# A planned attention and channel-mix kernel: longer warm-up of TensorE, two small loads requested elsewhere, a finer last piece, and a new order

## The chip, the core and the metric

The kernel runs on one core of one Trainium2 chip. The metric is the device time of one execution in microseconds (us). Three executions of the kernel before took 245.69, 247.63 and 247.31 us; their median is 247.31 us. A further execution was taken with the profiler; it took 246.16 us, of which the profile's span covers 244.4 us.

A core has five engines that run side by side, each through its own queue in order: PE (TensorE, the matmuls; its weight loads are listed as PEld), DVE (VectorE), ACT (ScalarE), POOL (GpSimd) and SP (SyncE, which here only requests transfers). They wait for each other through semaphores. Transfers run on 16 DMA engines of their own. PSUM, where matmuls write, has eight banks of 512 fp32 columns.

## The reference

Two layers, for 4 batches of 768 rows.

1. **Hashed attention**, 8 heads of 64 columns. `proj` (64 x 6) gives each row of q and k six sign bits, `bits = (q @ proj > 0)`. A row of q sees only rows of k whose six bits are the same: `scores = where(same, q @ k.T / 8, -1e9)`, `attn = softmax(scores)`, `x = attn @ v`. The heads side by side make 512 columns.
2. **Channel mix.** `xk = mu_k * x + (1 - mu_k) * x_prev`, `xr` likewise with `mu_r`, where `x_prev` is x one row earlier. `out = sigmoid(xr @ w_r) * (relu(xk @ w_k)^2 @ w_v)`, with w_k 512 x 1024, w_v 1024 x 512, w_r 512 x 512. The output is 4 x 768 x 512 in fp32.

## The kernel before, in words

**Units of work.** Two heads of one batch make a pair, so there are 16 pairs, `n` = 0 to 15, four to a batch. For a pair, q and k are loaded, scaled and split into a high and a low fp16 half (`hi`, `lo` on DVE: L456 and L461 for pairs 0 and 1, L393 and L396 for the others), and transposed. Pairs 0 and 1 are transposed by PE against the identity `idh` (`t...`, L474) and copied out of PSUM (`evt...`, L479 on DVE, L481 on ACT); the others are transposed by a DMA (L400, requested by SP).

**Hash bits.** `proj` is loaded into `pj` (L260). POOL makes `npj = -pj` (L261), the fp16 high part `p1` (two copies, L264) and the low part `p2` (two subtractions, L267). PE multiplies the transposed rows with `p1` and `p2`: in two halves for the first head of pair 0 (`b0...`, L494), else a pair at a time (`bits...`, L420). The signs become six extra rows of the transposed q and k: `beb...` for the first head of pair 0 (L500 on ACT for k, L502 on DVE for q), else `bx` on DVE (L423) and then a copy by POOL (`row...`, L440). With them the score matmul itself tells equal from unequal bits.

**Scores and values.** `sc{n}_{s}` (L533) is one of nine steps of 1024 score columns of a pair; ACT takes its exponential (`exp{n}_{s}`, L537, 144 in all). `oo{n}_{j}` (L560, with L555 for pairs 0 to 3) multiplies by v; DVE divides (`rc`, `ob`, L571 to L578). The result is transposed into `xt` and mixed on DVE (`df`, `xka`, `xk`, `xra`, `xr`, L598 to L633). The sums over v are POOL's (`vsum`, L351 to L357), and so are the casts of v for pairs 0 to 3 (`va`, L345) and of the weights to bf16 (`wc`, L303).

**Channel mix of a batch**, after its four pairs: `kp` (L648) with a relu on ACT (L652) and a square on DVE (L655); `r` (L668) with a tanh on ACT (L671); then, for each of six chunks of 128 rows, `v` (L681), the product on DVE (`os`, L688), and the store, requested by SP (`st`, L691). The last chunk of the last batch is done in two pieces of 256 columns, each with its own matmuls, product and store.

**Order.** Every step is recorded by `add(engine, duration, function, ...)` and numbered in the order of the calls. The list `ORDER` holds these numbers in the order in which the steps are issued; an engine runs its own steps in that order. `BANKS` gives the PSUM bank of each step that takes one. Both lists are written out in the file. The durations and due times (`dur`, `at`, `svc`) in the `add` calls are not used when the program is built from these lists.

In the numbering of the kernel before, 0 is the zeroing of `wz`, 2 to 8 are seven warm-up matmuls of 512 columns (L246), 10 and 11 make the identities `idh` and `idb` (two POOL instructions each), 12 to 24 are POOL's memsets, 25 requests `pj` on ACT's queue, and 26 to 30 are the five POOL steps that make `npj`, `p1` and `p2`. POOL's steps start in the order 18, 13, 20, 12, 14, 11, 19, 10, 1, 15, 26, 27, 28, 29, 30; then comes `va0`.

Of the kernel before, what the change touches and what calls it, by code (L numbers as in the profile page):

```python
# [13 lines left out]
ALU = mybir.AluOpType  # L14
# [113 lines left out]
def kernel(  # L128
# [19 lines left out]
    P = 128  # L148
# [6 lines left out]
    NPB = H // 2  # L155
    NPAIRS = B * NPB

    NWARM = 7
    NUC = 4
    FIRST = {(n, side, j): ("DVE", "DVE", None) for n in range(2) for side in "qk" for j in range(2)}  # L160
    FIRST[(0, "q", 0)] = ("DVE", "DVE", "DVE")
# [534 lines left out]
    for n in range(NPAIRS):  # L696
        if n == 0:
            for m in range(2):
                add_load(m)
# [48 lines left out]
```

## Time and profile before

| what | value |
|---|---|
| three executions | 245.69, 247.63, 247.31 us (median 247.31) |
| the profiled execution | 246.16 us; span 244.4 us |
| busy: PE, DVE, ACT, POOL | 233.1, 189.4, 180.7, 103.8 us |
| first exponential on ACT | 14.12 us |
| PE's last matmuls begin | 239.21 us |
| last product on DVE | 241.16 us, 0.42 us long |
| `pj` requested, landed | 1.17 us, 4.0 us later |

The profile lists, for one execution, when each engine ran what. Times are counted from the start of the span. "Idle before" is the time that an engine stood still ahead of an instruction, and the name behind the arrow is what ended it. A line of the timeline stands for several instructions of one form in a row; its second number reaches from the first's start to the last's end. Matmuls overlap, so a line of PE is about 0.17 us longer than the work in it, and lines overlap by as much.

### The profile page before, as it was taken

The page shows a single profiled execution, that of the slowest core. Times are in us where ns is not written, and L with a number is a line of the kernel's source. Part 1 is how long each engine was busy: PE and PEld are TensorE (multiplying, and loading weights), DVE is VectorE, ACT ScalarE, POOL GpSimd, SP SyncE. Part 2 cuts the span into 40 slices and gives each one's busy share as a digit, 9 for nine tenths or more (in the row PEclk, how much of TensorE's full clock was granted, in tenths as well). Part 3 has the DMA queues.
Part 4 walks back from the last instruction along what each step waited for, and adds up shares of the span by engine and source line. Part 5 has one row for each costly group of instructions (what it writes and reads, how often), then busy time and mean ns, then how long its engine had stood idle before and what let it go on. Part 6 is the DMA issues. An engine that isn't in the chain of part 4 may idle for free.

```text
span 244.4 us, 6114 instructions
## 1 busy us (share of the span) xinstructions
PE 233.1 (95%) x2461; PEld 140.5 (57%) x2461; DVE 189.4 (77%) x392; ACT 180.7 (74%) x241; POOL 103.8 (42%) x151
## 2 busy tenths in 40 slices
PE   6899998999999989999999999999999999999994
PEld 3455565675666645555766665565557575455443
DVE  3998779899997999997898989975246837873342
ACT  3469999899999895688887886886979970156320
POOL 3479989599947694116087030770040000000000
PEclk9999999999999999999999999999999999999999
DMA  7999999999999999999999794265102101321033
GB/s 228 343 248 189 242 249 186 343 198 362 291 248 245 265 376 195 178 278 325 187 198 238 203 200 135 60 160 120 32 1 89 32 3 35 129 85 45 3 130 129
DMA packets 72381, 43.99 MB, mean 180 GB/s; under 512 B 54816, under 2 KB 67360, under 8 KB 72352
## 3 DMA queue, kind: packets, MB, share of 16 engines
q1 hardware_dynamic: 72128, 43.40, 72.7%
q8 instruction: 19, 0.31, 0.6%
q10 hardware_dynamic: 224, 0.20, 0.3%
q14 instruction: 10, 0.08, 0.1%
HBM read 24.12 MB, written 6.29 MB: 124 GB/s over the span
## 4 chain that ended last, share of the span: by engine, by line
PE 60%; DVE 1%; issue 0%
PE ps_all L681 16%; PE ps_all L648 13%; PE ps_all L533 13%; PE ps_all L560 8%; PE ps_all L668 8%; PE ps_all L420 2%; DVE tm L630 0%; DVE os L688 0%; DVE ob L578 0%; PE ps_all L369 0%; PE ps_all L588 0%; PE ps_all L370 0%
## 5 line engine op out<-in xcount | busy, mean ns | idle before, releaser
L537 ACT ACTIVATE pt<-ps_all 128x1024 bf16<-128x1024 f32 x144 | 140.6, 1041 | 22.4 <-PE ps_all L533 21.4
L533 PE MATMUL ps_all<-a 128*128 128x256 f16 (+1 forms) x384 | 82.0, 326 | 0.5
L440 POOL COPY a<-bx 6x384 f32<-6x384 f32 x62 | 45.3, 731 | 58.2 <-DVE bx L423 35.1
L648 PE MATMUL ps_all<-xk,wk 128*128 128x384 bf16 x256 | 48.8, 326 | 0.1
L560 PEld LDWEIGHTS <-pt 128*128 128x128 bf16 x1152 | 43.2, 97 | 9.5 <-issue 1.4
L681 PE MATMUL ps_all<-wv,k 128*128 128x512 bf16 (+1 forms) x200 | 46.7, 370 | 0.8 <-DVE ob L578 0.8
L533 PEld LDWEIGHTS <-a 128*128 128x128 f16 x384 | 32.8, 97 | 24.2 <-issue 5.5
L560 PE MATMUL ps_all<-va,pt 128*128 128x65 bf16 x1152 | 45.3, 193 | 0.0
L655 DVE TENSOR_TENSOR k<-kr 128x384 bf16<-128x384 bf16 x64 | 24.8, 404 | 15.5 <-ACT kr L652 13.3
L652 ACT ACTIVATE kr<-ps_all 128x384 bf16<-128x384 f32 x64 | 30.0, 500 | 9.0 <-PE ps_all L648 7.2
L648 PEld LDWEIGHTS <-wk 128*128 128x128 bf16 x256 | 24.6, 98 | 17.2 <-POOL wk L303 0.4
L681 PEld LDWEIGHTS <-k 128*128 128x128 bf16 x200 | 19.0, 98 | 19.3 <-issue 1.1
L671 ACT ACTIVATE rs<-ps_all 128x512 f32<-128x512 f32 x24 | 14.3, 603 | 21.2 <-PE ps_all L668 17.8
L396 DVE SCALAR_TENSOR_TENSOR nh<-nat,nh 128x1536 f16<-128x1536 f32 (+1 forms) x16 | 26.6, 1662 | 0.3
L668 PE MATMUL ps_all<-wr,xr 128*128 128x512 bf16 x96 | 24.5, 379 | 0.2 <-DVE ob L578 0.2
L688 DVE SCALAR_TENSOR_TENSOR os<-rs,ps_all 128x512 f32<-128x512 f32 (+1 forms) x25 | 16.5, 661 | 9.8 <-PE ps_all L681 9.3
L423 DVE TENSOR_SCALAR bx<-ps_all 128x768 uint16<-128x768 uint16 (+1 forms) x16 | 15.2, 952 | 5.2 <-PE ps_all L420 4.3
L351 POOL TENSOR_TENSOR vt<-vn 128x384 f32<-128x384 f32 x12 | 15.0, 1253 | 8.3 <-DMA vn<-in_v_dram 7.7
L578 DVE TENSOR_TENSOR ob<-ps_all,rc 128x384 bf16<-128x384 f32 x32 | 17.3, 548 | 0.4
L393 DVE TENSOR_SCALAR nh<-nat 128x1536 f16<-128x1536 f32 (+1 forms) x16 | 15.3, 959 | 1.4 <-DMA nat<-in_q_dram 1.4
L420 PE MATMUL ps_all<-a,p 128*32 128x512 f16 (+1 forms) x248 | 14.2, 334 | 1.7 <-DMA a<-nh 0.8
L668 PEld LDWEIGHTS <-xr 128*128 128x128 bf16 x96 | 9.2, 98 | 10.4 <-issue 0.8
(72 smaller groups left out, 179.7 us busy)
## 6 DMA issues: line engine op xcount, KB each, us to landing
vn<-in_v_dram SPq DMA_DIRECT2D x16, 384.0 KB, 5.4
out_dram<-os SPq DMA_DIRECT2D x23, 256.0 KB, 2.2
nat<-in_q_dram SPq DMA_DIRECT2D x15, 384.0 KB, 5.3
nat<-in_k_dram SPq DMA_DIRECT2D x15, 384.0 KB, 5.1
wst<-in_moe_w_k_dram SPq DMA_DIRECT2D x2, 512.0 KB, 6.4
wst<-in_moe_w_r_dram SPq DMA_DIRECT2D x2, 512.0 KB, 4.3
wst<-in_moe_w_v_dram SPq DMA_DIRECT2D x2, 512.0 KB, 6.0
k<-in_moe_w_k_dram SPq DMA_DIRECT2D x1, 512.0 KB, 4.8
```

The lines of the kernel that those rows point to most:

```text
L396: nc.vector.scalar_tensor_tensor(out=nh[:, :, D:P], in0=nat.rearrange("p j (c d) -> p (j c) d", d=D), scalar=QS, in1=nh[:, :, 0:D], op0=AL ...
L420: nc.tensor.matmul(ps[32 * i : 32 * i + 32, lo:hi], w_, side_a[side][sa][:, j, lo:hi], start=st, stop=not st)
L440: nc.gpsimd.tensor_copy(side_a[side][sa][D : D + NB, j, :].bitcast(FP32), bx_t[sx][32 * i : 32 * i + NB, :].bitcast(FP32))
L533: nc.tensor.matmul(ps[:, lo - s * STEP : hi - s * STEP], side_a["k"][sa][:, j, jc * P : (jc + 1) * P], side_a["q"][sa][:, j, q0 : q0 + hi ...
L537: nc.scalar.activation(out=pt_t[sp][:, s * STEP : (s + 1) * STEP], in_=ps_t[plan.slot[nm]], func=AF.Exp, bias=EBIAS, scale=ESC)
L560: nc.tensor.matmul(oo[:, ic * 65 : ic * 65 + 65], pt_t[sp][:, o : o + P], va_t[sa][:, j, jc, 0 : D + 1], start=(not uc and ic == 0 and jc ...
L578: nc.vector.tensor_tensor(out=ob_t[so][:, :, j * D : (j + 1) * D], in0=oo[:, :, 0:D], in1=rc_t[sr][:, 1, :].unsqueeze(2).to_broadcast([P, ...
L648: nc.tensor.matmul(ps[:, 0:HALF], wk_sb[:, d, fc * P : (fc + 1) * P], xk_t[mx[d]][:, h * HALF : (h + 1) * HALF], start=(d == 0), stop=(d = ...
L652: nc.scalar.activation(out=kr_t[sk], in_=sm(nm)[:, 0:HALF], func=AF.Relu, scale=0.5 ** 0.5)
L655: nc.vector.tensor_tensor(out=k2_t[s2][:, h * HALF : (h + 1) * HALF], in0=kr_t[sk], in1=kr_t[sk], op=ALU.mult)
L668: nc.tensor.matmul(sm(nr), xr_t[mx[d]][:, c * P : (c + 1) * P], wr_sb[:, d, :], start=(d == 0), stop=(d == NDC - 1))
L681: nc.tensor.matmul(sm(nv)[:, x0:x1], k2_t[(b * NFC + fc) % NK2][:, c * P : (c + 1) * P], wv_sb[:, fc, x0:x1], start=(fc == 0), stop=(fc == ...
```

## The change

Five edits, all in one file.

- The seven warm-up matmuls of 512 columns become twenty of 256.
- The request of `pj` is no longer a step of its own: the step that requests the first k block on ACT's queue requests `pj` right behind it. The five POOL steps that use `pj` are recorded later (`add_proj`), after the loads of pairs 0 and 1.
- The due time of the two mix-vector loads `muk` and `mur` is raised from 0.75 to 9.0.
- The last chunk of the last batch is done in three pieces (256, 128 and 128 columns) instead of two of 256. The keys that order the uses of the `os` buffer follow.
- `ORDER` and `BANKS` are new throughout.

```diff
 ORDER = [
-    18, 13, 0, 20, 12, 14, 11, 19, 10, 2, 3, 4, 5, 6, 7, 8, 56, 60, 55, 57, 58, 25, 61, 96, 73, 83, 74, 84, 79, 75, 85, 102, 110, 103, 63,
-    59, 86, 95, 64, 1, 9, 76, 80, 87, 88, 158, 159, 31, 62, 65, 69, 111, 66, 89, 70, 106, 168, 114, 15, 26, 27, 28, 29, 30, 169, 81, 90, 67,
-    107, 82, 77, 78, 68, 71, 72, 91, 165, 92, 130, 131, 108, 126, 128, 104, 166, 170, 211, 124, 109, 127, 98, 16, 99, 115, 105, 112, 113,
...
+    64, 70, 23, 85, 63, 67, 62, 65, 0, 108, 68, 29, 107, 34, 86, 25, 30, 95, 96, 33, 26, 71, 1, 32, 37, 72, 36, 28, 2, 3, 4, 5, 6, 7, 8, 9,
+    10, 11, 12, 13, 14, 15, 66, 114, 16, 17, 18, 19, 122, 87, 20, 27, 35, 73, 74, 115, 75, 88, 69, 21, 97, 89, 99, 98, 76, 77, 100, 81, 91,
+    101, 123, 78, 82, 180, 126, 102, 118, 181, 92, 90, 83, 177, 79, 93, 103, 22, 94, 80, 84, 142, 104, 110, 111, 178, 143, 116, 138, 31,
...
-    NWARM = 7
+    NWARM = 20
...
-        add("PE", 0.43, lambda: nc.tensor.matmul(sm("warm"), wz[:, 0:P], wz, start=True, stop=True),
+        add("PE", 0.109, lambda: nc.tensor.matmul(sm("warm")[:, 0:256], wz[:, 0:P], wz[:, 0:256], start=True, stop=True),
...
-    add("ACT", 0.42, lambda: nc.scalar.dma_start(out=pj, in_=proj), w=["pj"], at=1.25, svc=0.05)
-    add("POOL", 0.2, lambda: nc.gpsimd.tensor_scalar(out=npj, in0=pj, scalar1=-1.0, scalar2=None, op0=ALU.mult), r=["pj"], w=["npj"])
...
-        add("SP", 0.5, f_mu, w=[key], at=0.75, svc=0.2, name=key)
+        add("SP", 0.5, f_mu, w=[key], at=9.0, svc=0.2, name=key)
...
+                        if lq == "ACT":
+                            nc.scalar.dma_start(out=pj, in_=proj)
...
-            cuts = ((0, 256), (256, 512)) if b == B - 1 and c == NSC - 1 else ((0, 512),)
+            cuts = ((0, 256), (256, 384), (384, 512)) if b == B - 1 and c == NSC - 1 else ((0, 512),)
...
+    def add_proj():
+        add("POOL", 0.2, lambda: nc.gpsimd.tensor_scalar(out=npj, in0=pj, scalar1=-1.0, scalar2=None, op0=ALU.mult), r=["pj"], w=["npj"])
...
     for n in range(NPAIRS):
         if n == 0:
             for m in range(2):
                 add_load(m)
+            add_proj()
             add_prep_first(0)
```

In the new numbering 2 to 21 are the warm-ups, 22 a one-element exponential on ACT (`table`, 9 before), 23 makes `idh`, 24 `idb`, 25 to 37 are POOL's memsets, 64 requests the first k block and `pj`, 70 makes `npj`, 71 and 72 `p1`, 73 and 74 `p2`, 75 is `hi0q0`. POOL's steps now start in the order 70, 23, 29, 34, 25, 30, 33, 26, 71, 1, 32, 37, 72, 36, 28, 27, 35, 73, 74; then comes `va0`. On PE, eighteen of the warm-ups stand ahead of the first transposes (87, `t0k00`) and the other two right behind them; then follow `t0q10`, `b0k00`, `t0q00`, `t0q01`, `t0k01`, `t0k10`, `b0q01`, `b0q00`, `b0k01`, `bits0` and the first score step `sc0_3`. Before, this stretch was `t0k01`, `t0k00`, `t0q10`, `t0q00`, `t0q01`, `t0k10`, `b0k01`, `b0q00`, `b0k00`, `b0q01`, `bits0`, `sc0_3`. On DVE the stretch was `hi0q1`, `lo0k0`, `lo0q1`, `hi1q0`, `hi1q1`, `lo1q0`, `hi0q0`, `evt0q10`, `lo0q0`, `lo0k1`, `lo1q1`, `evt0q00`, `evt0q01`, `hi1k0`, `hi2` (k), `hi1k1`, `lo2` (k), `lo1k0`, `beb0q00`, `beb0q01`, `hi2` (q), `bx0`, and is now `lo0k0`, `hi0q1`, `lo0q1`, `hi1q0`, `hi1q1`, `lo1q0`, `hi0q0`, `evt0q10`, `lo0q0`, `lo0k1`, `lo1q1`, `evt0q00`, `evt0q01`, `hi2` (k), `hi1k1`, `hi1k0`, `lo2` (k), `hi2` (q), `beb0q00`, `beb0q01`, `bx0`; `lo1k0` comes after `bx0`. The order of the exponentials of pairs 0 to 5 on ACT is unchanged. Further on, the order moves steps by up to a few us of PE work against each other; each batch's channel mix keeps its place among the pairs.

More of the change, by code (lines that the diff above doesn't have):

```diff
@@ L259 @@
         add("POOL", 0.1, lambda i=i: nc.gpsimd.memset(xt_t[i][:, 0:1], 0.0), w=[("xz", i)])
-    add("ACT", 0.42, lambda: nc.scalar.dma_start(out=pj, in_=proj), w=["pj"], at=1.25, svc=0.05)
-    add("POOL", 0.2, lambda: nc.gpsimd.tensor_scalar(out=npj, in0=pj, scalar1=-1.0, scalar2=None, op0=ALU.mult), r=["pj"], w=["npj"])
-    for e in range(2):
-        rows = slice(e * D, (e + 1) * D)
-        add("POOL", 0.2, lambda rows=rows: nc.gpsimd.tensor_copy(p1[rows, 0:NB], npj), r=["npj"], w=["p1"])
-    for e in range(2):
-        rows = slice(e * D, (e + 1) * D)
-        add("POOL", 0.2, lambda rows=rows: nc.gpsimd.tensor_tensor(
-            out=p2[rows, 0:NB], in0=npj, in1=p1[0:D, 0:NB], op=ALU.subtract), r=["npj", "p1"], w=["p2"])
     for t, src, key in ((muk, moe_mu_k, "muk"), (mur, moe_mu_r, "mur")):
@@ L288 @@
             stage = os_all[:, 0 : 2 * DM]
-            keys = [("os", i, h) for i in range(2) for h in (0, 256)]
+            keys = [("os", i, h) for i in range(2) for h in (0, 256, 384)]
         else:
@@ L321, in f @@
                                       in_=SRC[side][b, 2 * t + j].rearrange("(p c) d -> p (c d)", c=NSC))
-                    add(lq, 0.42, f, at=0.75, w=[("nat", side, s, j)], svc=0.5, name=f"ldq{n}{side}{j}")
+                        if lq == "ACT":
+                            nc.scalar.dma_start(out=pj, in_=proj)
+                    add(lq, 0.42, f, at=0.75, w=[("nat", side, s, j)] + (["pj"] if lq == "ACT" else []), svc=0.5, name=f"ldq{n}{side}{j}")
             else:
@@ L691, in st @@
                     nc.sync.dma_start(out=out[b].rearrange("(p c) m -> c p m", c=NSC)[c][:, x0:x1], in_=os_t[so][:, x0:x1])
-                wo = [("os", so, h) for h in (0, 256) if x0 <= h < x1]
+                wo = [("os", so, h) for h in (0, 256, 384) if x0 <= h < x1]
                 add("DVE", DVE_C(x1 - x0), fo, r=[(nv,), ("rs", s1)], w=wo, give=[nv], name=f"os{b}_{c}_{x0}")
                 add("SP", 0.45, st, r=wo, svc=0.65 * (x1 - x0) / 512, name=f"st{b}_{c}_{x0}")
+    def add_proj():
+        add("POOL", 0.2, lambda: nc.gpsimd.tensor_scalar(out=npj, in0=pj, scalar1=-1.0, scalar2=None, op0=ALU.mult), r=["pj"], w=["npj"])
+        for e in range(2):
+            rows = slice(e * D, (e + 1) * D)
+            add("POOL", 0.2, lambda rows=rows: nc.gpsimd.tensor_copy(p1[rows, 0:NB], npj), r=["npj"], w=["p1"])
+        for e in range(2):
+            rows = slice(e * D, (e + 1) * D)
+            add("POOL", 0.2, lambda rows=rows: nc.gpsimd.tensor_tensor(
+                out=p2[rows, 0:NB], in0=npj, in1=p1[0:D, 0:NB], op=ALU.subtract), r=["npj", "p1"], w=["p2"])
     for n in range(NPAIRS):
```

2 lines of the change are left out of this document (1 added, 1 removed), and 113 rows, old and new, of tables (BANKS, ORDER).

## The prediction

> **What bounds the kernel now.** I read the busy times of the page first, then sums over three stretches, then the timelines of ACT and of the start.
>
> ```profile
> PE 233.1 (95%) x2461; PEld 140.5 (57%) x2461; DVE 189.4 (77%) x392; ACT 180.7 (74%) x241; POOL 103.8 (42%) x151
> ...
> PE 60%; DVE 1%; issue 0%
> ```
>
> PE carries the chain that ended last. But the first 62 us have another limit, as the stretches show (us; busy PE, PEld, DVE, ACT, POOL; clock; DMA share; GB/s):
>
> ```profile
> 14.00:62.00 48.00, 44.62 (x625) 29.16 (x624) 43.07 (x67) 45.87 (x50) 41.95 (x53) 1.00 1.14 253
> 62.00:200.00 138.00, 136.48 (x1533) 84.22 (x1530) 112.92 (x247) 115.67 (x156) 55.57 (x75) 1.00 0.75 177
> 200.00:242.00 42.00, 41.12 (x261) 21.83 (x259) 23.28 (x57) 14.11 (x28) 0.00 (x0) 1.00 0.22 77
> ```
>
> Until batch 0 has its four pairs, no channel mix can fill PE, and ACT's exponentials run end to end. ACT's timeline says it best:
>
> ```profile
> 14.12 3.77 ACT L537 ACTIVATE pt<-ps_all 128x1024 bf16<-128x1024 f32 x4 [2.39 <-PE ps_all L533]
> 18.57 25.47 ACT L537 ACTIVATE pt<-ps_all 128x1024 bf16<-128x1024 f32 x27 [0.68 <-PE ps_all L533]
> 44.99 16.89 ACT L537 ACTIVATE pt<-ps_all 128x1024 bf16<-128x1024 f32 x18 [0.95 <-PE ps_all L533]
> ```
>
> 49 exponentials with two gaps, 0.68 and 0.95 us. So the first one, at 14.12, sets the pace for everything behind: a slip of the start reaches 62 us except for what the gaps swallow, and then PE has 1.5 us of idle time in 138 and 0.9 in 42, so it can't win a slip back. The profiled execution took 246.16 us, 1.15 less than the median of 247.31. My sum is a difference against it, which I add to the median. No difference under 1% (2.5 us) can be told from none here.
>
> **The start: POOL now waits for `proj` ahead of the identity.** This is the part I weigh most.
>
> ```profile
> 1.62 0.21 POOL masks.py:197 MEMSET idh<- 128x128 f16 x1
> 1.89 0.29 POOL masks.py:199 TENSOR_SCALAR_AFFINE_SELECT idh<-idh 128x128 f16<-128x128 f16 x1
> ...
> 5.26 0.50 POOL L261 TENSOR_SCALAR npj<-pj 64x6 f32<-64x6 f32 x1 [2.89 <-DMA pj<-in_proj_dram]
> 5.83 0.67 POOL L264 CAST p<-npj 64x6 f16<-64x6 f32 x2
> 6.58 0.44 POOL L267 TENSOR_TENSOR p<-npj,p 64x6 f16<-64x6 f32 x2
> ```
>
> Before, the identities and memsets are done in the time that `pj` travels; `npj` then waits for it until 5.26. In the new list POOL's first step is `npj`. `pj` is requested as before, second on ACT's queue behind the k block (1.17 us, landing 4.0 us later), so joining the two requests buys nothing and `npj` again starts at about 5.26. Everything of POOL is queued behind it. `idh`: 5.26 + 0.57 (start to start, 5.26 to 5.83) + 0.27 + 0.29 = 6.39 instead of 2.18. Then twelve memsets at 0.07 (five took 0.73 to 1.07), two copies 0.75, two subtractions 0.44: `p2` is ready at about 8.4 instead of 7.02.
>
> PE's first transposes began at 5.04 and were held by DVE; now `t0k00` starts at 6.45. With three transposes at 0.107, two warm-ups at 0.21 and six transposes, `t0q10` ends near 7.85 and `evt0q10` can start at 8.05 on DVE, which had run it at 6.64. DVE's seven steps ahead of it, 4.43 to 6.91, contain no wait, so DVE stands still for 1.1 us. That hurts because DVE was without a pause here: from `evt0q10` (6.64) to the end of `beb0q01` (12.53) it needs 5.9 us. The new list takes `lo1k0` out of this stretch (0.5) and puts `hi2` of q in (0.5, or 1.03 as at 12.55 beside a POOL cast): `beb0q01` ends at 13.9 to 14.45. The first score step was PE's to start (13.18, behind half-rate bits), now it is DVE's, at 13.95 to 14.5; its exponential followed 0.94 later at half rate, some 0.6 at full: 14.55 to 15.1, a slip of **0.4 to 1.0**.
>
> Pair 1 comes next. From the end of `beb0q01` to `bx1` (19.38) lay 6.85; without `hi2` and with `lo1k0` 6.3, so `bx1` starts at 20.2 to 20.8, **0.8 to 1.4** late. Its copies on POOL and `sc1_2` (22.48) fed an exponential without a gap at 23.1, so this is ACT's slip too; I take 1.0. The gap at 44 us ends with the landing of a DMA transpose that is itself paced by transfers (DVE waits 1.20 for a q block at 31.78); it can swallow up to 0.95. I take 0.4, and **+0.6** reaches 62 us (ends -0.1 and +1.4).
>
> **Warm-ups.** Seven at 0.427 take 3.17 us. Eighteen at half that take 3.84 from 1.19, so they end at 5.03, ahead of the transposes in either case, and the two others fill PE's new wait. Cost: 0. Whether they raise the rate is the question. The clock row shows 9 throughout, so the half rate has to be read from durations:
>
> ```profile
> 9.11 2.74 PE L494 MATMUL ps_all<-a,p 128*32 128x384 f16 x8
> ...
> 13.92 0.50 PE L474 MATMUL ps_all<-idh,nh 128*128 128x128 f16 x6
> ```
>
> 384 columns take 0.32 us, 1.2 columns per ns, at 9 us; six transposes of 128 at 13.92 take 0.056 each, twice that rate. So the gate opened at 13 to 14 us, after 6 us of steady matmuls, and the first 3.17 us had not opened it. The Trainium skill (TensorE: Matmul & The Clock Gate, Part 1) says that about 3.4 us of sustained activity in a free-running window open it; by that rule 4.3 us may open it at some 5 to 8 us, if the window falls well. What early opening would give: four `b0` steps and `bits0` took 4.1 us of PE and would take half, 2 us. But the first score step would still wait for DVE at 13.95, as above, so in my sum it is worth 0; without POOL's wait it would be worth PE's lag behind `beb0q01`, 0.66, and 0.34 on the score step, 1.0 in all.
>
> **The last chunk.** Product and store of the last piece are what is left after PE.
>
> ```profile
> 241.16 0.42 DVE L688 SCALAR_TENSOR_TENSOR os<-rs,ps_all 128x256 f32<-128x256 f32 x1 [0.40 <-PE ps_all L681]
> ```
>
> 512 columns take 0.69 and 256 take 0.42, so 128 take 0.29: -0.13. Stores of 256 KB land in 2.2, of 128 KB in 1.7; at 64 KB I estimate 1.6: -0.1. The third request (0.33) fits between pieces 0.45 apart. Eight more short matmuls are the same columns: +0.03. Sum **-0.2** (0 to -0.4).
>
> **The rest of the order.** The mix vectors: only the place counts. `mur` took SP 1.55 us; it moves ahead of pair 3's transposes, which wait for DVE's `lo3` anyway, and both vectors are needed only at 30 us: 0. The one-element exponential moves between `beb` steps, 0.19 on an ACT that waits there: 0; were a second table load (1.28) put in with it, it would fall at 12 us, ahead of the first exponential. In the PE-bound stretches all that can be won is the waits that PE shows: DVE's products and quotients held it for 0.8, 0.5 and 0.2 us past 62 us, **-1.5**. What can be lost is a bank that DVE returns late. The chain shows one such link at 153.57 to 155.9, through `os`, `tm` and `ob`, 2.3 us long: **+2.3** is the other end. The new list keeps every batch's place, moves `mean12` and `mean13`, and with them three DVE steps each, some 11 us of PE work later, the latter out of DVE's fullest stretch, and brings other DVE steps closer to their users. I see no side that outweighs, and take 0.
>
> **Sum:** +0.6 - 0.2 + 0 = +0.4: 246.6 for a profiled execution, **247.7** for the median.
>
> **Rivals.**
> - *As summed*, 247.7, 0.48.
> - *DVE becomes the bound in the channel mix (slower).* From 90 to 160 us DVE is busy 64.8 of 70 (9.4, 9.9, 7.8, 9.6, 9.1, 9.1, 9.8 in steps of ten). If the new list asks for its products earlier, PE waits for banks; this decides once DVE's 5.2 us of slack there shrink by about the length of one link. One more link: +0.4 + 2.3 = +2.7, 250.0. For it: a single such link shows now. Against it: `mean13` moved out of that stretch. 0.25.
> - *The start and the order both win (faster).* `pj` lands early enough not to hold POOL and the gate opens early: first exponential 1.0 earlier; the three DVE waits go: -1.5; tail -0.2. Together -2.7, 244.6. Against it: the 4.0 us of `pj`. 0.17.
> - *The change does nothing.* POOL isn't held, the gate stays as it was, the orders are equal: tail alone, -0.2, 247.1. 0.10.
>
> Within 1% lie the first and the last: 0.58; faster 0.17, slower 0.25. A range of 245.0 to 250.2 leaves the outer halves of both outer cases out.
>
> **What would show it.** `npj` first on POOL at about 5.2, `idh` after 6, the first transpose at 6.4 or later, a DVE wait of about 1 us for `t0q10`, the first exponential at 14.5 to 15.1 the first one of pair 1 with a gap before it; the last product 0.29 us long. A first transpose at 5 us, 0.107 turning to 0.056 per transpose before 9 us, or PE idle of more than 2 us past 62 us would make it wrong.

## The result and the profile after

The kernel after takes **250.78 us** (median of six runs, 247.96 to 251.38); the kernel before, run beside it, takes 247.23 us (six runs, 245.69 to 248.26). The ratio is 1.0122, with a 95% interval of 1.0083 to 1.0162. Ratios here and below leave out executions more than 1.5% above the fastest of their kernel. The prediction was 247.7 us with a range of 245.0 to 250.2. The profiled execution after took 250.78 us with a span of 249.0, against 246.16 and 244.4 before, 4.62 us more.

Three lines of the page of the kernel after: busy time by engine, the clock row (tenths of full speed in 40 slices), and the shares of the chain that ended last.

```profile
PE 233.5 (94%) x2463; PEld 142.8 (57%) x2482; DVE 195.2 (78%) x393; ACT 181.3 (73%) x241; POOL 106.2 (43%) x151
...
PEclk9989999999999999999999999999999999999999
...
PE 63%; DVE 27%; issue 5%; POOL 2%; ACT 1%; DVEq 0%; POOLq 0%
```

PE does the same work (233.5 us of busy time, 233.1 before), so the time was lost standing still. DVE has 27% of the chain. That can't be set beside its 1% in the kernel before, because the chain of that kernel can be followed back only to 91 us, and this one to the start. But it tells where DVE holds the kernel after: from 14 to 76 us the chain stands on DVE for 47 of 62 us. From 91 us on it stands there for 15 us, against 2.8 before. The clock row has one 8, in its third slice, where the kernel before had only 9s.

The stretches of the kernel after (window; length; busy PE, PEld, DVE, ACT, POOL; clock; DMA share; GB/s): first the three stretches that the prediction shows for the kernel before, then three short ones.

```profile
14.00:62.00 48.00, 43.56 (x606) 28.48 (x607) 44.78 (x67) 43.22 (x47) 37.61 (x45) 0.96 1.02 238
62.00:200.00 138.00, 134.09 (x1452) 82.30 (x1463) 115.70 (x243) 115.11 (x156) 62.87 (x79) 1.00 0.74 177
200.00:242.00 42.00, 41.68 (x317) 23.05 (x322) 23.91 (x63) 17.30 (x31) 0.00 (x0) 1.00 0.21 75
...
13.10:16.45 3.35, 1.11 (x13) 0.53 (x8) 3.29 (x7) 0.67 (x2) 0.00 (x0) 1.00 0.70 180
16.55:19.90 3.35, 3.03 (x18) 2.08 (x18) 3.15 (x5) 2.33 (x3) 2.71 (x4) 0.50 0.64 122
19.95:23.30 3.35, 3.12 (x37) 1.77 (x35) 3.18 (x5) 3.02 (x4) 1.69 (x3) 1.00 0.99 247
```

In the first stretch ACT works 43.22 us instead of 45.87: the start is late. In the second PE works 134.09 of 138 us instead of 136.48: something is lost there too. The short stretches show the clock: full from 13.1 on, half from 16.5 to 19.9, full again. In the stretch ahead of the half rate, PE worked only 1.11 of 3.35 us.

ACT's timeline of the kernel after, the exponentials (start, length, count, and in brackets the idle time before and what ended it):

```profile
16.52 1.02 ACT L531 ACTIVATE pt<-ps_all 128x1024 bf16<-128x1024 f32 x1 [2.50 <-PE ps_all L527]
18.56 1.94 ACT L531 ACTIVATE pt<-ps_all 128x1024 bf16<-128x1024 f32 x2 [1.02 <-PE ps_all L527]
20.83 2.85 ACT L531 ACTIVATE pt<-ps_all 128x1024 bf16<-128x1024 f32 x3 [0.34 <-PE ps_all L527]
24.04 1.02 ACT L531 ACTIVATE pt<-ps_all 128x1024 bf16<-128x1024 f32 x1 [0.35 <-PE ps_all L527]
25.21 36.89 ACT L531 ACTIVATE pt<-ps_all 128x1024 bf16<-128x1024 f32 x39
```

The first exponential comes at 16.52 instead of 14.12, and three gaps of 1.02, 0.34 and 0.35 us follow. The first lies in the half-rate stretch, the others right behind it. The 46th exponential ends at 62.10; before, it ended at 58.90. I use that moment below to cut the time in two, **start** (up to it) and **rest** (from it to the end of the execution). Before: 58.90 and 187.26. After: 62.10 and 188.68. So the start lost 3.20 us and the rest 1.42.

How the start came late, in three timelines. POOL's:

```profile
5.12 0.24 POOL L691 TENSOR_SCALAR npj<-pj 64x6 f32<-64x6 f32 x1 [4.68 <-DMA pj<-in_proj_dram]
...
5.59 0.30 POOL masks.py:199 TENSOR_SCALAR_AFFINE_SELECT idh<-idh 128x128 f16<-128x128 f16 x1
...
7.99 1.07 POOL L697 TENSOR_TENSOR p<-npj,p 64x6 f16<-64x6 f32 x2
10.93 0.82 POOL L339 CAST va<-vn 128x768 bf16<-128x768 f32 x1 [1.86 <-DMA vn<-in_v_dram]
```

PE's:

```profile
5.94 0.48 PE L468 MATMUL ps_all<-idh,nh 128*128 128x128 f16 x3 [0.73 <-POOL idh masks.py:199]
...
9.12 0.50 PE L488 MATMUL ps_all<-a,p 128*32 128x384 f16 x1 [1.01 <-POOL p L697]
9.55 1.78 PE L468 MATMUL ps_all<-idh,nh 128*128 128x128 f16 x15
...
15.89 0.59 PE L527 MATMUL ps_all<-a 128*128 128x512 f16 x3 [2.24 <-DVE a L496]
```

DVE's, with the last product of the kernel at its end:

```profile
10.09 0.68 DVE L473 COPY a<-ps_all 128x384 f16<-128x384 f16 x2 [0.61 <-PE ps_all L468]
11.37 0.80 DVE L387 TENSOR_SCALAR nh<-nat 128x768 f16<-128x768 f32 x1 [0.60 <-PE ps_all L468]
12.08 1.35 DVE L450 TENSOR_SCALAR nh<-nat 128x384 f16<-128x384 f32 x2
...
14.81 1.03 DVE L496 TENSOR_SCALAR a<-ps_all 6x384 uint16<-6x384 uint16 x2
...
245.78 0.29 DVE L682 SCALAR_TENSOR_TENSOR os<-rs,ps_all 128x128 f32<-128x128 f32 x1 [0.16 <-PE ps_all L675]
```

Three lines of DVE in the kernel before, to compare: the copies behind the second transposes, `hi2` of k, and the signs.

```profile
8.52 0.61 DVE L479 COPY a<-ps_all 128x384 f16<-128x384 f16 x2
9.31 0.55 DVE L393 TENSOR_SCALAR nh<-nat 128x768 f16<-128x768 f32 x1
11.50 1.03 DVE L502 TENSOR_SCALAR a<-ps_all 6x384 uint16<-6x384 uint16 x2
```

Read them in this order. POOL starts with `npj` and waits 4.68 us for `pj`. The identity is late, so PE's first transposes run at 5.94. `p2` is done at 9.06, two microseconds later than before. PE stands at `b0k00`, the first hash-bit step, until 9.12, and **15 transposes stand behind it in PE's queue**. Their copies on DVE (10.09) wait, then `hi2` of k (11.37) waits, because it overwrites a buffer that the last of these transposes reads. Two small steps then take 1.35 us beside POOL's work, and the signs `beb0q00` and `beb0q01` (14.81) end at 15.84, 3.3 us later than before. PE's first score step waits 2.24 us for them (13.65 to 15.89), and at 16.50 the clock closes.

In the rest, PE's waits past 62 us (total, number and longest, in us) begin with these:

```profile
PE ps_all L414 <- DVE mc L376: 1.7, 1, 1.7
PE ps_all L527 <- DVE bx L417: 0.7, 1, 0.7
```

`bits7` at 75.99 waits 1.65 us for `mc5`, a DVE step of one column that gives back the PSUM bank which `bits7` takes.

### The profile page after: what moved, and what is told of

Its sections match the earlier page's. It is cut to its first block, busy times and chain, and to the rows that moved or that the text cites. A ratio compares the mean times of both kernels' runs of the same rounds, so it can differ in the third digit from the quotient of the medians.

```text
span 249.0 us, 6146 instructions
## 1 busy us (share of the span) xinstructions
PE 233.5 (94%) x2463; PEld 142.8 (57%) x2482; DVE 195.2 (78%) x393; ACT 181.3 (73%) x241; POOL 106.2 (43%) x151
## 4 chain that ended last, share of the span: by engine, by line
PE 63%; DVE 27%; issue 5%; POOL 2%; ACT 1%; DVEq 0%; POOLq 0%
PE ps_all L675 15%; PE ps_all L642 14%; PE ps_all L527 14%; PE ps_all L554 8%; PE ps_all L662 7%; DVE nh L390 4%; DVE nh L387 3%; DVE bx L417 3%; PE ps_all L414 3%; DVE ob L572 2%; DVE k L649 2%; DVE df L613 1%; DVE xk L618 1%; DVE xr L618 1%; PE ps_all L468 1%
## 5 line engine op out<-in xcount | busy, mean ns | idle before, releaser
L527 PE MATMUL ps_all<-a 128*128 128x512 f16 (+1 forms) x384 | 81.8, 328 | 3.7 <-DVE a L496 2.2
L527 PEld LDWEIGHTS <-a 128*128 128x128 f16 x384 | 33.9, 98 | 27.7 <-issue 7.2
L675 PE MATMUL ps_all<-wv,k 128*128 128x512 bf16 (+2 forms) x197 | 46.0, 362 | 0.6
L649 DVE TENSOR_TENSOR k<-kr 128x384 bf16<-128x384 bf16 x64 | 28.6, 466 | 16.6 <-ACT kr L646 16.4
L390 DVE SCALAR_TENSOR_TENSOR nh<-nat,nh 128x1536 f16<-128x1536 f32 (+1 forms) x16 | 27.8, 1735 | 0.2
L682 DVE SCALAR_TENSOR_TENSOR os<-rs,ps_all 128x512 f32<-128x512 f32 (+2 forms) x26 | 16.7, 643 | 12.6 <-PE ps_all L675 9.3
L662 PE MATMUL ps_all<-wr,xr 128*128 128x512 bf16 x88 | 23.1, 379 | 0.8 <-DVE ob L572 0.4
L417 DVE TENSOR_SCALAR bx<-ps_all 128x768 uint16<-128x768 uint16 (+1 forms) x16 | 15.2, 949 | 2.1 <-PE ps_all L414 1.2
L414 PE MATMUL ps_all<-a,p 128*32 128x512 f16 (+1 forms) x248 | 13.9, 331 | 1.9 <-DVE mc L376 1.7
```

Of the source, the lines that this page charges most:

```text
L390: nc.vector.scalar_tensor_tensor(out=nh[:, :, D:P], in0=nat.rearrange("p j (c d) -> p (j c) d", d=D), scalar=QS, in1=nh[:, :, 0:D], op0=AL ...
L417: nc.vector.tensor_scalar(out=bx_t[sx][0:rows].bitcast(U16), in0=ps_t[plan.slot[nm]][0:rows, 0:S].bitcast(U16).rearrange("p (c e) -> p c e ...
L527: nc.tensor.matmul(ps[:, lo - s * STEP : hi - s * STEP], side_a["k"][sa][:, j, jc * P : (jc + 1) * P], side_a["q"][sa][:, j, q0 : q0 + hi ...
L649: nc.vector.tensor_tensor(out=k2_t[s2][:, h * HALF : (h + 1) * HALF], in0=kr_t[sk], in1=kr_t[sk], op=ALU.mult)
L662: nc.tensor.matmul(sm(nr), xr_t[mx[d]][:, c * P : (c + 1) * P], wr_sb[:, d, :], start=(d == 0), stop=(d == NDC - 1))
L675: nc.tensor.matmul(sm(nv)[:, x0:x1], k2_t[(b * NFC + fc) % NK2][:, c * P : (c + 1) * P], wv_sb[:, fc, x0:x1], start=(fc == 0), stop=(fc == ...
```

## Experiments

The table gives the medians, and for the profiled execution of each the first exponential, the end of the 46th (start) and what comes behind (rest), in us. Kernels `b...` are built on the kernel before, all others on the kernel after.

| kernel | median | profiled | first exp | start | rest |
|---|---|---|---|---|---|
| before | 247.23 | 246.16 | 14.12 | 58.90 | 187.26 |
| `b1_proj_first` | 248.42 | 248.15 | 15.32 | 60.89 | 187.26 |
| `b2_warm20` | 246.77 | 246.38 | 13.42 | 59.14 | 187.24 |
| after | 250.78 | 250.78 | 16.52 | 62.10 | 188.68 |
| `a1_proj_behind` | 246.41 | 245.04 | 13.48 | 57.14 | 187.90 |
| `a1_again` | 246.90 | 247.25 | 14.30 | 58.51 | 188.74 |
| `a2_fill_wait` | 249.44 | 249.75 | 16.64 | 60.94 | 188.81 |
| `a3_b0_behind` | 249.78 | 250.07 | 16.22 | 61.38 | 188.69 |
| `a4_proj_request` | 251.58 | 251.80 | 17.82 | 63.35 | 188.45 |
| `d1_warm7` | 248.84 | 248.39 | 15.10 | 59.49 | 188.90 |
| `c1_split_behind` | 247.80 | 248.72 | 12.66 | 60.19 | 188.53 |
| `c2_bx0_first` | 249.19 | 248.73 | 12.38 | 60.13 | 188.60 |
| `c3_mc5_early` | 246.46 | 249.24 | 15.96 | 60.41 | 188.83 |
| `a5_mc5_early` | 250.60 | 250.47 | 16.89 | 61.53 | 188.94 |

The last column was the surprise: with the old list it is 187.24 to 187.26, whatever the start, and with the new list 187.90 to 188.94. One profile stands out: that of `c3_mc5_early` is the longest of its twelve executions, 2.8 us above their median, and its start (60.41) holds two half-rate stretches, listed below.

The kernel before, run beside these on the same chips, had medians of 246.88 (for `b1`, `b2`, `a1_proj_behind` and `a2`), 246.96 (`a3`, `a4`, `c1`, `d1`), 247.09 (`c2`, `a1_again`) and 246.99 (`c3`, `a5`).

### Is it POOL's wait? `a1_proj_behind` and `b1_proj_first`

Once undone in the kernel after, and once done alone in the kernel before. In `a1_proj_behind` the steps `npj` and `p1` go back behind POOL's identity and memsets:

```diff
-    64, 70, 23, 85, ... 33, 26, 71, 1, 32, 37, 72, 36, ... 27, 35, 73, 74,
+    64, 23, 85, ... 33, 26, 1, 32, 37, 36, ... 27, 35, 70, 71, 72, 73, 74,
```

> The changed kernel, with the first three POOL steps that use proj (npj and the two copies of p1) moved behind the identity and the memsets; nothing else. If POOL's wait at the start is the loss (theory 1): idh is ready near 1.6 us, the first transpose starts at 5.1 instead of 5.9, p2 is ready at about 7 instead of 9.1, so b0k00 no longer holds the transposes behind it, PE has no second-long pause before the first score step and its clock stays up; first exponential at 14 to 14.5 instead of 16.5, pair 1's first at 23.5 to 24.5 instead of 27.2, time 247.5 to 248.5. If the loss lies in the rest of the new order, in its banks or later stages (theory 2): the start improves as said but the time stays at 249.8 or more.

In `b1_proj_first`, the kernel before with the k request, the `pj` request, `npj` and `idh` at the front of the list:

```diff
-    18, 13, 0, 20, 12, 14, 11, 19, 10, 2, 3, ... 57, 58, 25, 61, ... 15, 26, 27,
+    57, 25, 26, 10, 18, 13, 0, 20, 12, 14, 11, 19, 2, 3, ... 58, 61, ... 15, 27,
```

> The kernel before, with npj as POOL's first step and the identity idh right behind it, as in the changed kernel; PE's, ACT's and DVE's orders and the banks are those of before. Theory 1, POOL's wait alone: idh at 5.9 us, first transpose at 6, first exponential 1 to 1.5 us later than 14.1, time +1 to +2, 248.3 to 249.3. Theory 2: the start slips by under 0.5 at 62 us, time within 0.5 of before. If the first exponential slips by about 1.4 and not 2.4, the other 1.0 of the changed kernel comes from its PE and DVE orders at the start.

Measured: `a1_proj_behind` 246.41 us (245.04 to 248.88; ratio to before 0.9974, 0.9949 to 0.9998). Its exponentials:

```profile
13.48 1.02 ACT L531 ACTIVATE pt<-ps_all 128x1024 bf16<-128x1024 f32 x1 [2.03 <-PE ps_all L527]
14.79 7.66 ACT L531 ACTIVATE pt<-ps_all 128x1024 bf16<-128x1024 f32 x8 [0.29 <-PE ps_all L527]
22.77 36.50 ACT L531 ACTIVATE pt<-ps_all 128x1024 bf16<-128x1024 f32 x39 [0.32 <-PE ps_all L527]
```

`b1_proj_first` 248.42 us (247.66 to 248.91; ratio 1.0049, 1.0029 to 1.0068):

```profile
15.32 3.77 ACT L537 ACTIVATE pt<-ps_all 128x1024 bf16<-128x1024 f32 x4 [2.41 <-PE ps_all L533]
19.84 25.79 ACT L537 ACTIVATE pt<-ps_all 128x1024 bf16<-128x1024 f32 x27 [0.74 <-PE ps_all L533]
```

POOL's wait is the cause: three POOL steps put back recover 4.4 us, more than the whole loss. But its price depends on the list around it. Alone in the old list it costs 1.20 us at the first exponential and 1.5 in the time; in the new list it costs 3.04 and 4.4 (2.2 and 3.9 against `a1_again`, a repeat of `a1_proj_behind`). What makes the difference is the subject of the next runs.

### The clock: `a2_fill_wait` and `b2_warm20`

`a2_fill_wait` issues the hash-bit matmuls of pair 0 four times over, which keeps PE busy where it stood waiting; the repeats compute the same values again and are not part of the reference.

```diff
-            for w_, st in ((p1, True), (p2, False)):
+            for w_, st in ((p1, True), (p2, False)) * (4 if n == 0 else 1):
```

> The changed kernel, with pair 0's bits matmuls issued four times over instead of once (same result each time), so that PE works through its 2.2 us pause ahead of the first score step. If the clock that drops at 16.5 us and comes back at 19.9 costs time (theory 3): the first exponential stays at 16.5, no half rate after it, the ACT gap of 1.0 us behind the first exponential shrinks to under 0.4, and the time falls by 1.1 to 1.7, to about 249.3. If the clock does not matter: the slip of pair 1's first exponential stays at 4.1 and the time at 250.5 to 251.

`b2_warm20` gives the kernel before the long warm-up, in its seven steps:

```diff
+        def fw(i=i):
+            for _ in range(2 if i == NWARM - 1 else 3):
+                nc.tensor.matmul(sm("warm")[:, 0:256], wz[:, 0:P], wz[:, 0:256], start=True, stop=True)
-        add("PE", 0.43, lambda: nc.tensor.matmul(sm("warm"), wz[:, 0:P], wz, start=True, stop=True),
+        add("PE", 0.43, fw,
```

> The kernel before with its seven 512-column warm-ups replaced by twenty of 256 columns (4.3 us instead of 3.0), nothing else. If longer warm-up opens the clock early: transposes at 0.056 instead of 0.107 us each before 9 us, first exponential up to 1.0 earlier, time -0.5 to -1. If not: the last two warm-ups push the first transpose from 5.0 to about 5.5, time within 0.5 of before.

Measured: `a2_fill_wait` 249.44 us (246.47 to 250.03; ratio 1.0083, 1.0054 to 1.0113).

```profile
16.64 1.02 ACT L531 ACTIVATE pt<-ps_all 128x1024 bf16<-128x1024 f32 x1 [2.71 <-PE ps_all L527]
18.08 7.67 ACT L531 ACTIVATE pt<-ps_all 128x1024 bf16<-128x1024 f32 x8 [0.41 <-PE ps_all L527]
```

`b2_warm20` 246.77 us (246.03 to 249.07; ratio 1.0023, 0.9987 to 1.0059).

```profile
13.42 3.98 ACT L540 ACTIVATE pt<-ps_all 128x1024 bf16<-128x1024 f32 x4 [1.65 <-PE ps_all L536]
18.41 22.68 ACT L540 ACTIVATE pt<-ps_all 128x1024 bf16<-128x1024 f32 x24 [1.01 <-PE ps_all L536]
```

The trace records when the clock changes. Of the profiled executions (us; from, length, share of full speed; the stretch before the first entry is at half rate, and entries behind PE's last matmuls are left out):

```
before           13.82 232.11 1.0
b1_proj_first    13.14 232.11 1.0
after            13.08   3.41 1.0 | 16.50  3.41 0.5 | 19.91 228.69 1.0
a1_proj_behind    5.66 238.93 1.0
a1_again          5.69 238.93 1.0
a2_fill_wait      4.11   3.41 1.0 |  7.52  6.83 0.5 | 14.35 235.52 1.0
b2_warm20         4.78   3.41 1.0 |  8.20  3.41 0.5 | 11.61 232.11 1.0
a3_b0_behind     13.95   3.41 1.0 | 17.36  3.41 0.5 | 20.78 228.69 1.0
a4_proj_request   5.73   3.41 1.0 |  9.14 13.65 0.5 | 22.80 228.69 1.0
c1_split_behind   5.80  10.24 1.0 | 16.04  3.41 0.5 | 19.46 228.69 1.0
c2_bx0_first      4.09  13.65 1.0 | 17.74  3.41 0.5 | 21.16 225.28 1.0
d1_warm7         17.34 228.69 1.0
c3_mc5_early      4.74   3.41 1.0 |  8.15  3.41 0.5 | 11.57   3.41 1.0 | 14.98 3.41 0.5 | 18.39 228.69 1.0
a5_mc5_early      4.02   3.41 1.0 |  7.43 13.65 0.5 | 21.08 228.69 1.0
```

With PE kept busy the clock doesn't close at 16.5 (in this execution it closed earlier, from 7.52 to 14.35, and was open again before the first score step). The first exponential stays where it was, the first gap behind it shrinks from 1.02 to 0.41 us, and 1.3 us of the time come back (start 60.94 instead of 62.10). So the half-rate stretch in the kernel after is worth about a third of its loss. The executions of the two kernels overlap (247.96 to 251.38 and 246.47 to 250.03), so the size is less sure than the sign. The long warm-up alone opens the clock at 4.8 us in the old list, but a pause of 1.97 us (5.95 to 7.93) lets it close from 8.2 to 11.6, and the median gains nothing.

### PE's queue and the request: `a3_b0_behind` and `a4_proj_request`

`a3_b0_behind` is the kernel after with `b0k00` (89) moved behind the transposes that stood behind it:

```diff
-    97, 89, 99, 98, 76, 77, 100, 81, 91, 101, 123,
+    97, 99, 98, 76, 77, 100, 81, 91, 101, 89, 123,
```

> The kernel after with one step of PE moved: the first hash-bit step (`b0k00`, which needs `p2`) goes from ahead of `t0q00` ... `t0k10` to behind them, so that 15 transposes no longer stand behind the wait for `p2`. POOL still starts with `npj`. Theory (half of the 2.4 us slip of the first exponential is PE's queue standing behind `b0k00`, and `hi2` of k behind that): the first transposes still begin at 5.9, but the copies behind them start about 0.5 to 1.5 us earlier, the first exponential comes at 15.2 to 15.7 instead of 16.52, and the time is 249.0 to 249.9; should PE's pause before `sc0_3` shrink enough for the clock to stay open, 248.5. Rival (POOL's delay carries the whole slip, because `beb0q01` needs bits that need `p2` anyway): the first exponential stays at 16.3 to 16.6 and the time at 250.4 to 251.0.

`a4_proj_request` requests `pj` ahead of the first k block instead of behind it:

```diff
                     def f(side=side, j=j, lq=lq):
+                        if lq == "ACT":
+                            nc.scalar.dma_start(out=pj, in_=proj)
                         (nc.scalar if lq == "ACT" else nc.sync).dma_start(out=side_nat[side][s][:, j, :],
                                       in_=SRC[side][b, 2 * t + j].rearrange("(p c) d -> p (c d)", c=NSC))
-                        if lq == "ACT":
-                            nc.scalar.dma_start(out=pj, in_=proj)
```

> The kernel after with `pj` requested just ahead of the first k block on ACT's queue instead of just behind it; nothing else changes. Theory (what counts is when `pj` lands, since all of POOL waits for it): `pj` lands at 4.2 to 4.9 instead of 5.1, `npj`, `idh` and `p2` come earlier by as much (0.3 to 0.9), the k block lands about 0.4 later, the first exponential comes 0.2 to 0.8 earlier, and the time is 249.9 to 250.6. Rival (the landing is set by the other loads under way, not by the place in the queue): `npj` starts at 5.1 as before, the k block is later, and the time is 250.8 to 251.3.

Measured: `a3_b0_behind` 249.78 us (247.32 to 250.29; ratio 1.0075, 1.0045 to 1.0106). Its 15 transposes start at 8.85 instead of 9.55 and `hi2` at 10.67 instead of 11.37, though its `evt0q10` came 0.25 later. But then DVE's timeline reads

```profile
11.15 2.00 DVE L450 TENSOR_SCALAR nh<-nat 128x384 f16<-128x384 f32 x2
```

and ACT's

```profile
16.22 1.02 ACT L531 ACTIVATE pt<-ps_all 128x1024 bf16<-128x1024 f32 x1 [2.33 <-PE ps_all L527]
...
20.52 40.85 ACT L531 ACTIVATE pt<-ps_all 128x1024 bf16<-128x1024 f32 x43 [1.05 <-PE ps_all L527]
```

The queue was worth 0.7 us up to `hi2`, and two small steps gave 0.65 of it back: they took 2.00 us beside POOL's cast and sum (11.03 to 12.84), 1.35 in the kernel after, and 0.62 in `a1_proj_behind`, ahead of that cast. The time lies where the theory put it; the first exponential (16.22 against 15.2 to 15.7) doesn't, so the theory is right on the queue and half right on its worth.

`a4_proj_request` 251.58 us (249.61 to 252.18; ratio 1.0147, 1.0109 to 1.0186). POOL's timeline, then ACT's:

```profile
3.47 0.24 POOL L691 TENSOR_SCALAR npj<-pj 64x6 f32<-64x6 f32 x1 [3.03 <-DMA pj<-in_proj_dram]
```

```profile
6.39 0.52 ACT L452 ACTIVATE nh<-nat 128x384 f16<-128x384 f32 x1 [3.14 <-DMA nat<-in_k_dram]
```

`pj` landed 1.65 us earlier, as the theory wants and more, and the k block behind it, which `a4` was to delay by 0.4, 2.6 us later (6.39 against 3.76). DVE's first split step waited for it until 6.94, against 4.31. Both theories missed this; what it shows is that the place behind k costs POOL's start and the place ahead of it costs the k block.

### The warm-ups in the new list: `d1_warm7`

`a1_proj_behind` with the seven warm-ups of 512 columns (the list renumbered):

```diff
-    NWARM = 20
+    NWARM = 7
-        add("PE", 0.109, lambda: nc.tensor.matmul(sm("warm")[:, 0:256], wz[:, 0:P], wz[:, 0:256], start=True, stop=True),
+        add("PE", 0.109, lambda: nc.tensor.matmul(sm("warm"), wz[:, 0:P], wz, start=True, stop=True),
```

> The kernel `a1_proj_behind` (246.4) with the seven warm-up matmuls of 512 columns of the kernel before in place of the twenty of 256. Theory (the longer warm-up opened the clock at 5.7 us and it stayed open because PE's bits were no longer late): the clock opens at 12 to 14 us as in the kernel before, the bits take twice as long, the first exponential comes at 14.0 to 14.6, and the time is 246.8 to 247.6. Rival (the first score step waits for DVE, not for PE, so the warm-up is worth nothing): the first exponential at 13.4 to 13.7 and the time 246.2 to 246.7.

Measured: 248.84 us (247.16 to 249.44; ratio 1.0054, 1.0026 to 1.0082).

```profile
15.10 1.02 ACT L530 ACTIVATE pt<-ps_all 128x1024 bf16<-128x1024 f32 x1 [2.35 <-PE ps_all L526]
16.72 42.78 ACT L530 ACTIVATE pt<-ps_all 128x1024 bf16<-128x1024 f32 x45 [0.60 <-PE ps_all L526]
```

In the profile the clock opens only at 17.34, and 2.4 us are lost against `a1_proj_behind`, 1.9 against its repeat. Where POOL isn't late, the twenty warm-ups are worth as much as that in this list, more than the theory's 0.4 to 1.2; in the old list (`b2_warm20`) they are worth nothing.

### DVE's order at the start: `c1_split_behind`, `c2_bx0_first`, `a1_again`

In `a1_proj_behind` the bits of the first head were done 1.3 us before DVE came to them, as `lo2` of k (181) and `hi2` of q (177) stood ahead. `c1` moves these behind `beb0q01` (84), `c2` behind `bx0` (104) too:

```diff
-    118, 181, 92, 90, 83, 177, 79, 93, 103, 22, 94, 80, 84, 142, 104,
+    118, 92, 90, 83, 79, 93, 103, 22, 94, 80, 84, 181, 177, 142, 104,
```

```diff
-    118, 181, 92, 90, 83, 177, 79, 93, 103, 22, 94, 80, 84, 142, 104,
+    118, 92, 90, 83, 79, 93, 103, 22, 94, 80, 84, 142, 104, 181, 177,
```

> The kernel `a1_proj_behind` (the kernel after with `npj` and `p1` back behind the identity and the memsets, 246.4) with a further move on DVE: the second halves of pair 2's split of k (`lo2`) and the first of its split of q (`hi2`) go behind `beb0q00` and `beb0q01`, whose bits were done 1.3 us before DVE came to them. Theory (the start is now DVE's, and a gain of the first exponential lasts): the first exponential at 12.1 to 12.5 instead of 13.48, the time 245.2 to 245.8. Rival (pair 1 and pair 2 are paced by DVE as a whole and by transfers, so an earlier first score step only opens gaps behind it): first exponential as in the theory, but the gain is gone at pair 1 or pair 2, and the time is 246.2 to 246.7.

> As `c1_split_behind`, but `lo2` of k and `hi2` of q also go behind `bx0`, the signs of the second head, for which PE's second score step had waited 2.7 us in `c1_split_behind`. Theory (the start is DVE's: in `c1_split_behind` the two moved steps only changed places with `bx0`): the first exponential at 12.2 to 12.7, the gap behind it under 0.5 us, no half-rate stretch behind the opening of the clock, pair 1's first exponential 0.5 to 1.0 us earlier than in `a1_proj_behind`, and the time 0.4 to 1.0 below that kernel's on the same chip. Rival (pair 2's split, now later by 1.3 us, holds the scores of pair 1 or 2, as DVE has no pause here): the gain is gone by 30 us, and the time is that of `a1_proj_behind` within 0.4.

> The kernel `a1_proj_behind` once more, for comparison on the same chip as `c2_bx0_first`: if the clock is open without a break from 5 to 6 us on in nearly every run, as before, 246.1 to 246.7 and a narrow spread; if that hung on the phase of the first runs, 247 to 248 in several runs, each of them with a mean clock of 0.993 or less.

Measured: `c1_split_behind` 247.80 us (246.16 to 249.08; ratio 1.0015, 0.9986 to 1.0044).

```profile
12.66 1.02 ACT L531 ACTIVATE pt<-ps_all 128x1024 bf16<-128x1024 f32 x1 [0.72 <-PE ps_all L527]
16.36 1.94 ACT L531 ACTIVATE pt<-ps_all 128x1024 bf16<-128x1024 f32 x2 [2.68 <-PE ps_all L527]
```

`c2_bx0_first` 249.19 us (248.60 to 250.06; ratio 1.0094, 1.0059 to 1.0129), with this wait in PE's timeline:

```profile
16.53 0.51 PE L468 MATMUL ps_all<-idh,nh 128*128 128x128 f16 x6 [2.10 <-DVE nh L455]
```

`a1_again` 246.90 us (244.76 to 247.99; ratio 0.9983, 0.9954 to 1.0013).

The first exponential moved as expected (12.66 and 12.38 against 13.48 and 14.30), and none of it lasted: the gap came back as 2.68 us one step later, and in `c2` as 2.10 at pair 1's transposes, which wait for DVE's `lo1`. In both profiles the clock closed behind the pause, at 16.04 and 17.74. Of the twelve executions of `a1_again`, five have a mean clock of 0.993 or less and take 247.24 to 247.99, which comes near the second case named for it (a sixth takes 247.25 at 0.998). So the rival holds, and more than it said: an earlier first score with DVE full behind it is a longer pause for PE. `c2` is 2.3 us slower than `a1_again`, 1.5 of it in the profiled pair; where the rest of that lies isn't settled.

### The rest: `c3_mc5_early` and `a5_mc5_early`

`mc5` (490), 0.14 us long, goes from behind pair 8's split (601, 602) to behind `va5` (489), in `a1_proj_behind` (`c3`) and in the kernel after (`a5`):

```diff
-    488, 489, 569, 360, 523, 524, 525, 601, 602, 361, 490,
+    488, 489, 490, 569, 360, 523, 524, 525, 601, 602, 361,
```

> The kernel `a1_proj_behind` (246.41 and 246.90) with one DVE step of 0.14 us moved: `mc5`, which gives back the PSUM bank that `bits7` takes, goes from behind pair 8's split (`hi8`, `lo8`) and a square to directly behind `va5`. Theory (behind the start, the new list loses 1.65 us where `bits7` waits for `mc5`, and this is what the new order costs past 60 us): PE's wait of 1.65 at 72 to 76 us is gone; the profiled time less the end of the 46th exponential, which was 187.2 to 187.3 with the old list in three profiles and 187.9 to 188.9 with the new one in nine, falls by 1.0 to 1.7 to 187.0 to 187.8; the time is 245.0 to 245.8. Rival (PE then waits as long for the next step that DVE returns late, since DVE is behind as a whole there): PE waits for another DVE step within some 5 us, the rest stays at 188.2 to 188.9 and the time at 246.4 to 246.9.

> The kernel after with the same one step moved (`mc5` directly behind `va5`), its late start kept. Theory (the wait of `bits7` adds to the late start): no wait at 76 us, the rest behind the 46th exponential 187.0 to 187.8 instead of 188.68, the time 249.2 to 249.9 instead of 250.78. Rival as for `c3_mc5_early`: another DVE step takes the wait's place and the time stays at 250.4 to 251.0.

Measured: `a5_mc5_early` 250.60 us (249.57 to 250.67; ratio 1.0132, 1.0099 to 1.0165); `c3_mc5_early` 246.46 us (243.55 to 249.24, by far the widest spread; ratio 0.9947, 0.9913 to 0.9980). With that spread I don't take it for a gain over `a1_proj_behind` and `a1_again` (246.41 and 246.90). PE's longest wait past 57 us, the same line in `c3` and in `a5`:

```profile
PE ps_all L642 <- DVE ob L572: 1.4, 1, 1.4
```

The wait for `mc5` is gone in both, and at almost the same place PE now waits 1.44 us for `ob5`, the quotient that stands two steps behind it on DVE. The rest stays at 188.83 and 188.94. So it wasn't the one step: in the new list DVE as a whole comes some 1.5 us late to PE there. The 21.1 us behind the 46th exponential (window; length; busy PE, PEld, DVE, ACT, POOL; clock; DMA share; GB/s), before and after:

```profile
58.90:80.00 21.10, 20.63 (x229) 13.46 (x228) 19.05 (x37) 19.87 (x29) 15.52 (x20) 1.00 1.08 275
62.10:83.20 21.10, 19.45 (x253) 13.20 (x252) 20.76 (x36) 19.24 (x28) 17.87 (x20) 1.00 1.00 257
```

DVE is busy 20.76 us in the kernel after, in `a1_again` and in `c3`, and 19.05 before; PE works 19.45, 19.45 and 19.66 there, and 20.63 before. That is most of the difference of the rest. DVE has no more steps there, 36 against 37, but longer ones: nine squares (L649) take 6.23 us, where ten (L655) took 4.66. POOL is busier beside them, 17.87 us against 15.52. So the likely loss is that the new list sets DVE's squares beside POOL's steps; no run here moves them apart, and `ORDER` and `BANKS` were not separated.

## Why the prediction was wrong

The mechanism on which it put most weight was there, and its sign at the first exponential was right; its size was not. The order behind the start, set to 0, was +1.4, and for a clock that closes again the sum had no term. Point by point:

- **POOL's wait: the right mechanism up to `evt0q10`, and milder than said.** `npj` started at 5.12 (predicted 5.26), `idh` was ready at 5.89 (6.39), the transposes began at 5.94 (6.45), and `evt0q10` came 0.88 late (1.4), with DVE standing still for 0.28 us ahead of it (1.1). `p2` was later than said, 9.06 against 8.4, because POOL's steps became longer: the two subtractions, now beside three `lo` steps on DVE (8.00 to 9.48), took 1.07 us; they took 0.46 in `a4_proj_request`, where DVE stood idle, and 0.44 before.
- **"`beb0q01` ends at 13.9 to 14.45", slip 0.4 to 1.0: the step that failed.** It ended at 15.84 and the slip was 2.40. From the start of `evt0q10` to that end the sum had 5.9 to 6.4 us; it took 8.32, and 5.89 in `a1_proj_behind`, where POOL isn't late. The sum followed one engine, DVE, from `evt0q10` on as if nothing else could stop it, and DVE stood still twice for PE, 0.61 and 0.60 us. It left out PE's queue: `b0k00`, which needs `p2`, stands ahead of 15 transposes, whose copies were 1.57 us late, and `hi2` had to wait for the last transposes to read its buffer (+2.05). `b1_proj_first`, whose list has no hash-bit step ahead of transposes, slips by 1.20. `hi2` of k and the two `hi1` steps took 0.80 and 1.35 us beside POOL's cast and sum, 0.55 and 0.62 in `a1_proj_behind`: collisions that the sum had only for `hi2` of q. `a3_b0_behind` shows both: the queue's 0.7 us, and the collision that takes it back.
- **Pair 1 "+1.0", and "+0.6" at 62 us.** Pair 1's first exponential came 4.09 us late and the 46th ended 3.20 late. To the larger slip the half-rate stretch added its gaps (1.16 us of the 3.20, as `a2_fill_wait` has it). What the gap at 44 us swallowed was 1.0, against the 0.4 taken.
- **Warm-ups 0: wrong as a rule, about right in this kernel.** The prediction asked only when the clock opens, not whether it stays open. Behind POOL's wait the twenty warm-ups didn't open it early in the profile after (13.08); in `a2_fill_wait` and `a5_mc5_early`, whose start is as late, they opened it at 4.11 and 4.02, and it closed again at 7.52 and 7.43. DVE set the first score step, as said. But a late score step is a pause of PE, and behind the pause the clock closed. Without POOL's wait the same warm-ups open it at 5.7 us and are worth 1.9 to 2.4 (`d1_warm7`), where the prediction had 1.0.
- **The rest of the order 0, -1.5 to +2.3: +1.4.** Three profiles of the old list have 187.24 to 187.26 behind the 46th exponential, ten of eleven of the new one 188.45 to 188.94. The mechanism is that of the slower rival, DVE as the bound, but earlier (within 21 us of the 46th exponential, not at 90 to 160: there PE worked 68.78 of 70 us, 68.94 before), and as lateness of DVE as a whole, not as one link. That this rival's 250.0 lies near the 250.78 is luck: it had +2.3 in the order, where 1.42 were measured with the tail, and +0.6 in the start, where 3.20 were. "PE idle of more than 2 us past 62 us", named as what would make the prediction wrong, was there: 3.9 us up to 200.
- **Tail -0.2: about 0.** The last product took 0.29, as said, but from its end to the end of the span were 2.93 us, against 2.82.

The mix vectors' later requests were not run alone, and the tail is read from the profile only.

Sum in the profiled pair: start +3.20 instead of +0.6, rest +1.42 with the tail instead of -0.2: +4.62. In the medians +3.55.

## What to carry to other kernels

When a step is moved ahead of others on one engine, follow what it delays into every in-order queue that waits for it, one more engine than seems needed: here POOL delayed `p2`, `p2` stopped PE's queue, PE's queue stopped DVE's buffers, and DVE paused PE long enough for the clock to close. A first result that comes earlier is worth nothing if the engine that feeds the second is full; cut the time at a fixed event (here the 46th exponential) and compare both halves, since that tells a late start from a worse order in one look.

## What the runs showed of the hardware

- **The clock closes in fixed windows, and a pause far shorter than a window is enough.** All half- and full-rate stretches between changes are 3.41 us or whole multiples (6.83, 10.24, 13.65). In the kernel after it closed after a window in which PE worked 1.11 of 3.35 us, with a pause of 2.24; in `a2_fill_wait` after one with 1.50 of 3.41, where no pause was longer than 1.27. In `a1_proj_behind` a pause of 1.75 at 11.1 to 12.85, which the window boundary at 12.48 cuts in two, left it open, and in `a1_again` one of 2.11 (11.56 to 13.67), cut at 12.52. So PE's work in a window tells more than the length of a pause. In the profiles here, up to 24 us, the full-rate windows with 0.70 to 1.55 us of PE work were all followed by half rate; of those with 1.65 or more, only one was (1.98, in `c3_mc5_early`). Half-rate windows with 2.83 us or more were followed by full rate, those with 2.78 or less were not. The Trainium skill (TensorE: Matmul & The Clock Gate, Part 1) gives a free-running window of about 3.4 us for both directions, and the stretches agree. The Trainium skill (the same page, Why this matters for your kernels) advises against idle gaps of more than some 3 us; that is too mild here, where 2.24 was too long.
- **Where the window falls differs from run to run, and it shows in the time.** Each execution lists its mean clock (the stretch before the first opening counts as full there), and one closed window lowers it by about 0.007. Of the 24 executions of `a1_proj_behind` and its repeat, the 16 with a mean clock of 0.998 or more have a median of 246.28 us, the six with 0.993 of 247.68; `b2_warm20` 246.24 (five) and 247.49 (five), `c1_split_behind` 246.88 (four) and 248.40 (six). So in these kernels one closed window goes with 1.2 to 1.5 us more. That the window itself costs as much isn't shown, since where the windows fall also sets when the clock opens first. In the kernel before, with the old warm-up, the same split gives 246.95 (51 executions) and 246.94 (43): no difference.
- **The same DVE step can take three times as long beside POOL.** Two `hi1` steps took 0.62, 1.35 and 2.00 us. A square of the channel mix takes 0.35 us in the kernel after while POOL stands still (39 of the 64) and 0.59 to 1.24 in the five during which POOL works throughout; in the kernel before the five of that kind took 0.32 to 0.69, so it depends on what POOL does. The Trainium skill (SBUF — State Buffer, Who interferes with whom) says that VectorE and GpSimd share one pair of ports as a lock, held for a whole instruction; the trace agrees in that POOL's steps lengthen too (two subtractions 0.46 alone, 1.07 beside DVE).
- **With a request of 1.5 KB ahead of it on the same queue, a block of 192 KB landed 2.6 us later** (`a4_proj_request`), though the request itself took only 0.56 us to issue. The block was then requested at 1.34 us, behind SP's second q block (1.20), and landed behind it, so the small request or the lost place among the blocks may have held it; no run separates the two.
